# 384 columns of the down weights as a transfer with eight source stretches, and TensorE's loop waits held by its matmuls

## The chip, the cores and the metric

The kernel runs on one core of a Trainium2 chip. The core has a matrix engine (TensorE, PE in the profile, with its weight loads listed apart as PEld), a vector engine (VectorE, DVE), a scalar engine (ScalarE, ACT), GpSimd (POOL) and a sequencer that issues transfers (SyncE, SP). Sixteen DMA engines move data from the chip's main memory (HBM) into the on-chip buffer (SBUF); TensorE writes its results to PSUM. The engines run at once and order their work by counting semaphores. The metric is the device time of one execution in microseconds (us), less is better.

## The reference

One token is decoded through a layer: attention over a long cache, then a gated feed-forward block, each behind a layer norm and with a residual sum. Everything is float32.

```python
# D = 640, H = 32 heads, Sk = 8192 cached positions, Dh = 192, F = 1536
def _A_ref(x, k_cache, v_cache, wq, wo):
    q = (x @ wq) per head
    scores = einsum("bhqd,bhkd->bhqk", q, k_cache) * Dh ** -0.5
    p = softmax(scores)
    o = einsum("bhqk,bhkd->bhqd", p, v_cache)
    return o @ wo

def _B_ref(x, W_gate, W_up, W_down):
    gate = x @ W_gate
    h = gate * (gate > 0) * (x @ W_up)
    return h @ W_down

h  = x + _A_ref(layernorm(x), k_cache, v_cache, wq, wo)
h2 = h + _B_ref(layernorm(h), W_gate, W_up, W_down)
```

The caches of keys and values alone are 32 x 8192 x 192 x 4 bytes each, 403 MB together, and each byte is used once.

## The kernel before

The host packs every input into rows of 128 partitions (`pack`), in the order in which they are used, so that one transfer brings several things at once: a head's keys, values, columns of the query weights and rows of the output weights. Three large SBUF slots, X, Y and Z, take them.

**The loop.** After a first head's keys (`row_p`), ten turns of three heads each run. A turn uses five transfers, `row_1` to `row_5`, of 7.6 to 8.2 MB, which SP issues in `sync_program` (line 581): into X, Z, Y, X and Y. Before it issues one, it waits until the slot's old contents are used; TensorE, DVE and ACT report this on the semaphores `free`. `free[3]` lets the turn's last load into Y go (line 590). It takes two increments: one from the matmul of value block 23 of the turn's second head, and one that TensorE's sequencer sends after it has seen that DVE is done with Y (lines 250 to 252). A landed transfer adds 16 to its semaphore `land`.

**One head.** TensorE's part is `pe_unit` (line 226). It multiplies the head's keys by the query in two halves (`pe_k`, line 190), corrects the head before by its softmax sum (`pe_o`, `pe_l`), multiplies the values by the probabilities in 32 blocks (`pe_v`, line 197), makes the query of the next head (`pe_q`, line 206) and transposes a maximum (`pe_t`). ACT copies results out of PSUM and takes the exponential, and counts up `a2p` three times a head; DVE makes the softmax's maxima and the products with weights, and counts up `d2p` twice. `pe_unit` waits for these with `wait` (line 136): an instruction of its own on TensorE's sequencer, which takes what it waited for off the semaphore again. `op` (line 142) can hang a wait or an increment on a matmul instead. The waits for transfers (`landed`) are instructions of their own too.

**The tail.** After the last turn come the last head, the output product, the second layer norm, and the feed-forward block. Its weights arrive as `row_up`, `row_gate` and, by line 609, `row_down` in four pieces d0 to d3. The down weights are 12 rows of D = 640 columns on each partition, and the pieces are cut by `DOWN` (line 35):

```python
DOWN = ((0, 6 * D), (6 * D, 10 * D), (10 * D, 11 * D + D // 2), (11 * D + D // 2, 12 * D))
```

TensorE's last loop (line 326) goes over these rows j: it waits for d0 ahead of row 0, d1 ahead of row 6, d2 ahead of row 10, and d3 ahead of the second half of row 11. Rows 0 to 5 also need the first half of the transposed activations `guT`, which DVE makes (lines 503 and 505). `pe_fill` (line 258) is a matmul into an unused place, which keeps TensorE going ahead of a wait; one stands ahead of row 6. After the last row, ACT and DVE copy the result out of PSUM and SP stores it, as two rows of 320.

Of the kernel before, what the change touches and what calls it, by code (L numbers as in the profile page):

```python
# [11 lines left out]
DJ, FJ = D // P, F // P  # L12
# [19 lines left out]
W_T2B = 16 * PW  # L32
W_T3 = 16 * PW + OW
W_UP = DJ * F
DOWN = ((0, 6 * D), (6 * D, 10 * D), (10 * D, 11 * D + D // 2), (11 * D + D // 2, 12 * D))


def pack(inputs):
    import numpy as np
    order = np.arange(D).reshape(2, 2, DG).transpose(1, 0, 2).reshape(D)  # L40
    x = np.ascontiguousarray(inputs["A_x"]).reshape(D)[order].reshape(P, DJ)
    kc = np.ascontiguousarray(inputs["A_k_cache"])[0]
    vc = np.ascontiguousarray(inputs["A_v_cache"])[0].reshape(H, P, KW)
    wq = np.ascontiguousarray(inputs["A_wq"])[order].reshape(P, DJ, H, DH)
    wo = np.ascontiguousarray(inputs["A_wo"])[:, order].reshape(H, DH, D)

    def kt(h):
        k = kc[h].reshape(4, 32, 32, 2, DH).transpose(4, 3, 0, 2, 1).reshape(DH, 2, 4, 2, 512)
        a = k[:P]
        b = k[P:].transpose(1, 0, 2, 3, 4).reshape(P, 4, 2, 512)  # L50
        r = np.stack([a[:, 0], a[:, 1], b], 1)
        return r.transpose(0, 3, 1, 2, 4).reshape(P, KW)

    def qw(h):
        return wq[:, :, h].reshape(P, QW)

    def ow(h):
        w = wo[h]
        mid = w[DH - P:P]
        full = np.concatenate([w[:DH - P], w[P:]], 0)  # L60
        return np.concatenate([full, np.concatenate([mid[:, 0:D // 2], mid[:, D // 2:]], 0)], 1)

    cat = lambda *a: np.concatenate(a, 1)
    kw = [kt(h) for h in range(H)]
    out = {"row_p": cat(qw(0), kw[0], qw(1), x, np.zeros((P, W_P - 2 * QW - KW - DJ), np.float32))}
    rows = [np.empty((NTURN, P, w), np.float32) for w in (W_1, W_2, W_3, W_4, W_5)]
    for i in range(NTURN):
        a, b, c = 3 * i + 1, 3 * i + 2, 3 * i + 3
        va, vb, vv = vc[a - 1], vc[b - 1], vc[c - 1]
        rows[0][i] = cat(kw[a], va[:, :8 * PW], qw(b))  # L70
        rows[1][i] = cat(va[:, 8 * PW:], ow(a - 1), kw[b][:, :12 * 512])
        rows[2][i] = cat(kw[b][:, 12 * 512:], qw(c), vb[:, :24 * PW])
        rows[3][i] = cat(vb[:, 24 * PW:], kw[c])
        rows[4][i] = cat(ow(b - 1), ow(c - 1), qw(c + 1), vv)
    for n, r in enumerate(rows):
        out[f"row_{n + 1}"] = r
    h = H - 1
    out["row_t1"] = cat(kw[h], vc[h - 1][:, :8 * PW])
    out["row_t2a"] = cat(vc[h - 1][:, 8 * PW:], ow(h - 1))
    out["row_t2b"] = np.ascontiguousarray(vc[h][:, :16 * PW])  # L80
    out["row_t3"] = cat(vc[h][:, 16 * PW:], ow(h))
    out["row_up"] = np.ascontiguousarray(inputs["B_W_up"])[order].reshape(P, DJ * F)
    out["row_gate"] = np.ascontiguousarray(inputs["B_W_gate"])[order].reshape(P, DJ * F)
    down = np.ascontiguousarray(inputs["B_W_down"])[:, order].reshape(4, FJ, 32, D).transpose(0, 2, 1, 3).reshape(P, FJ, D)
    last = down[:, FJ - 1].reshape(P, 4, 2, DG // 2).transpose(0, 2, 1, 3).reshape(P, D)
    out["row_down"] = cat(down[:, :FJ - 1].reshape(P, (FJ - 1) * D), last)
    return {k: np.ascontiguousarray(v) for k, v in out.items()}


def build(nc, arrays):  # L90
# [51 lines left out]
    def op(ins, w=None, inc=None):  # L142
        if w is not None:
            ins._wait_ge(*w)
        if inc is not None:
            ins.then_inc(inc, 1)
        return ins
# [39 lines left out]

    te = nc.tensor

    def pe_k(blk, half):  # L190
        for part in range(3):
            for g in range(4):
                m = te.matmul(sc[Q(g), half * 512:half * 512 + 512], qs[:, 32 * part:32 * part + 32],  # L193
                              blk(half, part * 4 + g), start=(part == 0), stop=(part == 2))
        op(m, inc=p2d)

    def pe_v(blk, i0, i1, last=None, inc_at=None):
# [5 lines left out]
            if i == 31 and last is not None:  # L203
                op(m, inc=last)

    def pe_q():
        te.matmul(q_ps[:, 0:96], prod[:, 0:P], pat[:, 0, :], start=True, stop=False)  # L207
        te.matmul(q_ps[0:64, 0:96], prod[:, P:DH], pat[:, 1, :], start=False, stop=True)
        op(te.matmul(q_ps[64:P, 0:96], prod[:, P:DH], pat[:, 2, :], start=False, stop=True), inc=p2a)  # L209

# [12 lines left out]
    def pe_l(w=None):  # L223
        op(te.matmul(pl[:, 0:1], ones, vec["rs"], start=True, stop=True), w, inc=p2d)  # L224

    def pe_unit(kblk, vblk, rows, freed=None, freed_at=None, o_first=False):
        def landed(n):
            if n in rows:
                s, sub = rows[n]
                wait(te, s, 16, sub)  # L230

        wait(te, a2p, 1, 1)
        if o_first:
            wait(te, a2p, 1, 1)
            pe_o()
        landed("k0")
        pe_k(kblk, 0)
        if not o_first:
            wait(te, a2p, 1, 1)
            pe_o()  # L240
        wait(te, a2p, 1, 1)
        pe_l()
        landed("k1")
        pe_k(kblk, 1)
        landed("v0")
        at = None if freed is None else (freed_at, freed)
        pe_v(vblk, 0, 8, inc_at=at)
        landed("v8")
        pe_v(vblk, 8, 24, inc_at=at)
        wait(te, d2p, 2, 2)  # L250
        if freed is free[3]:
            te.sem_inc(freed, 1)
        pe_q()
        pe_t()
        landed("v24")
        pe_v(vblk, 24, 32, last=p2a)
# [4 lines left out]
    def tensor_program():  # L261
# [11 lines left out]
        wait(te, d2p, 2, 2)  # L273
        pe_q()
        pe_t()
        def first():
            pe_unit(ka, va, {"k0": (land[1], 16), "v8": (land[2], 16)}, free[1], 7, o_first=True)

        def rest():
            pe_unit(kb, vb, {"k1": (land[3], 16), "v24": (land[4], 16)}, free[3], 23)  # L280
            pe_unit(kc, vcc, {"v0": (land[5], 0)})

        turns(ET.PE, first, rest)
        pe_o((a2p, 2))
        pe_l((a2p, 3))
        wait(te, tl["t2b"], 16, 16)
        pe_v(vz, 0, 16)
        for g in range(4):
            op(te.matmul(acc[Q(g), 0:DG], ones[:, 0:32], accs[:, g * DG:(g + 1) * DG], start=True, stop=False),
               None if g else (d2p, 3))  # L290
        for g in range(4):
            r = slice(0, 64) if g < 2 else slice(64, P)
            te.matmul(acc[Q(g), 0:DG], ones[r, 0:32], accs[r, D + (g % 2) * DG:D + (g % 2 + 1) * DG],
                      start=False, stop=False)
        wait(te, tl["t3"], 16, 16)
        pe_v(vz, 16, 32, last=p2a)
        pe_o((a2p, 4))
        for g in range(4):
            op(te.matmul(acc[Q(g), 0:DG], oc[:, 0:1].to_broadcast([P, 32]), woz[:, g * DG:(g + 1) * DG],
                         start=False, stop=False), None if g else (d2p, 5))  # L300
        for g in range(4):
            r = slice(0, 64) if g < 2 else slice(64, P)
            m = te.matmul(acc[Q(g), 0:DG], oc[r, 1:2].to_broadcast([64, 32]),
                          woz[r, D + (g % 2) * DG:D + (g % 2 + 1) * DG], start=False, stop=True)
        m.then_inc(p2a, 1)
        op(te.matmul(pt[:, 0:1], ones, vec["hs1"], start=True, stop=True), (a2p, 5), inc=p2d)
        op(te.matmul(od[:, 0:1], ones, vec["hs2"], start=True, stop=True), (d2p, 6), inc=p2d)
        wait(te, tl["up"], 16, 16)
        for j in range(DJ):
            for g in range(4):  # L310
# [9 lines left out]
        op(m, inc=p2d)  # L320
        te.matmul(q_ps[:, 0:DG], ident, h4, start=True, stop=False)
        pe_fill(128)
        wait(te, a2p, 5, 5)
        wait(te, tl["d0"], 16, 16)
        wait(te, d2p, 7)
        for j in range(FJ):
            if j == 6:
                pe_fill(512)
                wait(te, d2p, 8, 8)
                wait(te, tl["d1"], 16, 16)  # L330
            if j == 10:
                wait(te, tl["d2"], 16, 16)
            if j < FJ - 1:
                for g in range(4):
                    te.matmul(q_ps[Q(g), 0:DG], guT[:, j, :], down[:, j * D + g * DG:j * D + (g + 1) * DG],  # L335
                              start=False, stop=False)
            else:
                for half in range(2):
                    if half:
                        wait(te, tl["d3"], 16, 16)  # L340
                    for g in (2, 3, 0, 1):
                        at = j * D + half * (D // 2) + g * (DG // 2)
                        m = te.matmul(q_ps[Q(g), half * (DG // 2):(half + 1) * (DG // 2)], guT[:, j, :],  # L343
                                      down[:, at:at + DG // 2], start=False, stop=bool(half))
                        if half and g == 3:
                            op(m, inc=p2a)
# [231 lines left out]
    def load(t, src, s):  # L578
        sp.dma_start(t, src).then_inc(s, 16)

    def sync_program():
# [24 lines left out]
        load(Y[:, W_T3:W_T3 + W_UP], dram["row_up"], tl["up"])  # L606
        wait(sp, free[1], 1, 1)
        load(X[:, 0:W_UP], dram["row_gate"], tl["gate"])
        for n, (a, b) in enumerate(DOWN):
            load(X[:, W_UP + a:W_UP + b], dram["row_down"][:, a:b], tl[f"d{n}"])  # L610
        wait(sp, fout, 2)
        load(out[0, 0].rearrange("(g n) -> g n", g=2), o2[31:33, :], out_s)
        wait(sp, fout, 2, 2)
# [22 lines left out]
```

## Time and profile before

| | |
|---|---|
| median of 3 runs | 1037.62 us (1037.56 to 1037.63) |
| the profiled execution | 1037.69 us |
| its span, first to last instruction | 1036.4 us |
| mean clock granted to TensorE | 0.76 of full |
| bytes moved by DMA in the span | 446.05 MB, 430 GB/s |

The profile is of one execution, 0.07 us above the median. Its busy times are those of work proper; waits, branches and the issuing of transfers count as idle. A letter q behind an engine (PEq) means its sequencer. L137 is line 137 of the kernel, the wait instruction inside `wait`; a row that names it as what ended an idle time means that the engine stood at such a wait, and the cause lies behind it. TensorE's float32 matmul is listed as two passes, so that the numbers of matmuls in the rows are twice those in the code.

### The profile page before, as it was taken

What the parts mean: (1) busy time and instruction counts of PE and PEld (TensorE: products, weight loads), DVE (VectorE), ACT (ScalarE), POOL (GpSimd) and SP (SyncE); (2) the same over time, 40 slices, a digit from 0 to 9 for tenths busy, and PEclk for the clock granted to TensorE, in tenths of its full rate; (3) what the DMA queues carried; (4) which work ended last, traced back from release to release, by engine and by line L of the source; (5) the groups of instructions that cost most, each with busy time, mean ns of one, the idle gap of its engine ahead of it and who ended that gap; (6) DMA issues with size and microseconds to landing.
All of it is one profiled execution on the core that took longest, in us unless ns stands there. A gap on an engine that the chain in (4) does not pass through costs nothing. (4 is left out here: it accounts for less than half of the span.)

```text
span 1036.4 us, 10124 instructions
## 1 busy us (share of the span) xinstructions
PE 549.5 (53%) x4374; PEld 185.5 (18%) x4374; DVE 196.0 (19%) x517; ACT 41.7 (4%) x139; POOL 1.5 (0%) x13
## 2 busy tenths in 40 slices
PE   0745546446364463564654636546455455464577
PEld 0211212111121121121211202111111111121123
DVE  1311211121222022121211210221222012111221
ACT  1000000000000000000000000000000000000000
POOL 0000000000000000000000000000000000000000
PEclk9877867768777677687676877867778778677788
DMA  9999999999999999999999999999999999999998
GB/s 403 442 435 421 434 438 432 441 421 438 427 451 416 436 445 437 416 441 437 438 421 442 431 438 435 421 438 441 427 425 438 439 423 434 438 432 444 420 425 352
DMA packets 8796, 446.05 MB, mean 430 GB/s; under 512 B 979, under 2 KB 1109, under 8 KB 1237
## 3 DMA queue, kind: packets, MB, share of 16 engines
q1 hardware_dynamic: 8788, 445.95, 99.6%
q8 instruction: 6, 0.10, 0.0%
q14 instruction: 2, 0.01, 0.0%
HBM read 445.94 MB, written 0.00 MB: 430 GB/s over the span
## 5 line engine op out<-in xcount | busy, mean ns | idle before, releaser
L193 PE MATMUL sc<-slot_x,qs 128*32 128x512 f32 x1008 | 150.7, 742 | 93.2 <-PEq L137 93.2
L200 PE MATMUL po<-slot_y,p 128*2 128x384 f32 x1152 | 118.2, 562 | 80.6 <-DMA slot_y<-row 76.8
L200 PE MATMUL po<-slot_z,p 128*2 128x384 f32 x560 | 72.0, 667 | 100.2 <-PEq L137 100.2
L193 PE MATMUL sc<-slot_y,qs 128*32 128x512 f32 x288 | 53.5, 905 | 83.0 <-PEq L137 83.0
L200 PE MATMUL po<-slot_x,p 128*2 128x384 f32 x336 | 43.6, 652 | 86.6 <-PEq L137 86.6
L406 DVE STREAM_TRANSPOSE st<-sc 128x512 f32<-128x512 f32 x64 | 45.6, 713 | 160.7 <-PE sc L193 160.7
L193 PEld LDWEIGHTS sc<-slot_x,qs 128*32 128x32 f32 x1008 | 36.7, 134 | 175.8 <-issue 175.5
L200 PEld LDWEIGHTS po<-slot_y,p 128*2 128x2 f32 x1152 | 31.0, 94 | 165.4 <-DMA slot_y<-row 85.9
L393 DVE COPY oc<-od 64x2 f32<-64x2 f32 x33 | 5.0, 151 | 246.6 <-PE od L218 246.6
L412 DVE TENSOR_REDUCE m<-pt 128x1 f32<-128x128 f32 x32 | 9.3, 292 | 185.6 <-PE pt L212 185.6
L200 PEld LDWEIGHTS po<-slot_z,p 128*2 128x2 f32 x560 | 15.2, 102 | 146.5 <-issue 145.2
L524 ACT COPY qs<-q_ps 128x96 f32<-128x96 f32 x33 | 7.9, 239 | 793.8 <-PE q_ps L209 793.8
L218 PE MATMUL od<-mrl,ob 128*128 128x1 f32 x264 | 35.2, 254 | 8.5 <-PEq L137 7.3
L218 PEld LDWEIGHTS od<-mrl,ob 128*128 128x128 f32 x264 | 32.8, 195 | 34.5 <-issue 31.2
L387 DVE SCALAR_TENSOR_TENSOR prod<-slot_y,xn,prod 128x192 f32<-128x192 f32 x88 | 36.9, 419 | 3.1
L193 PEld LDWEIGHTS sc<-slot_y,qs 128*32 128x32 f32 x288 | 12.7, 154 | 112.2 <-issue 112.2
L401 DVE RECIPROCAL rl<-pl 128x1 f32<-128x1 f32 x32 | 5.4, 168 | 134.1 <-PE pl L224 133.5
L200 PEld LDWEIGHTS po<-slot_x,p 128*2 128x2 f32 x336 | 9.0, 94 | 109.6 <-issue 109.6
L193 PE MATMUL sc<-slot_z,qs 128*32 128x512 f32 x240 | 27.6, 592 | 0.0
L527 ACT COPY ob<-po 128x384 f32<-128x384 f32 x32 | 15.3, 479 | 155.6 <-PE po L200 155.6
L207 PE MATMUL q_ps<-pat,prod 128*128 128x96 f32 x66 | 15.8, 322 | 7.1 <-PEq L137 7.1
L385 DVE TENSOR_SCALAR prod<-slot_y,xn 128x192 f32<-128x192 f32 x22 | 6.9, 315 | 64.7 <-DMA slot_y<-row 64.7
(97 smaller groups left out, 248.7 us busy)
## 6 DMA issues: line engine op xcount, KB each, us to landing
slot_x<-row SPq DMA_DIRECT2D x10, 8160.0 KB, 26.6
slot_z<-row SPq DMA_DIRECT2D x10, 8160.0 KB, 45.4
slot_y<-row SPq DMA_DIRECT2D x10, 8160.0 KB, 45.4
slot_x<-row SPq DMA_DIRECT2D x10, 7680.0 KB, 46.6
slot_y<-row SPq DMA_DIRECT2D x10, 7584.0 KB, 27.2
slot_x<-row_t SPq DMA_DIRECT2D x1, 7680.0 KB, 26.1
slot_y<-row_p SPq DMA_DIRECT2D x1, 7136.0 KB, 19.7
slot_z<-row_t2a SPq DMA_DIRECT2D x1, 5088.0 KB, 37.7
```

Of the source, the lines that this page charges most:

```text
L193: m = te.matmul(sc[Q(g), half * 512:half * 512 + 512], qs[:, 32 * part:32 * part + 32], blk(half, part * 4 + g), start=(part == 0), stop=( ...
L200: m = te.matmul(po[32 * g:32 * g + 2, 0:PW], p[:, 2 * i:2 * i + 2], blk(i), start=(i < 4), stop=(i >= 28))
L207: te.matmul(q_ps[:, 0:96], prod[:, 0:P], pat[:, 0, :], start=True, stop=False)
L218: m = te.matmul(od[:, part:part + 1], ob[:, at:at + P], mrl[:, k:k + 1], start=(k == 0), stop=(k == 1))
L385: dv(ve.tensor_scalar(prod, w3[:, 0, :], xn[:, 0:1], None, op0=ALU.mult), w=first)
L387: dv(STT(prod, w3[:, j, :], xn[:, j:j + 1], prod, op0=ALU.mult, op1=ALU.add), w="self", inc=d2p if j == DJ - 1 else None)
L393: dv(ve.tensor_copy(oc[0:64], od[0:64, 0:2]), w=pd(), inc=inc)
L401: dv(ve.reciprocal(vec["rl"], pl[:, 0:1]), w=pd())
L406: return dv(ve.transpose(st[:, s], sc[:, s]), w=w)
L412: dv(ve.reduce_max(vec["m1"], pt[:, 0:P], axis=AX.X, negate=True), w=pd(), inc=d2a)
L524: op(ac.copy(qs, q_ps[:, 0:96]), w=ap("p2a"), inc=a2p)
L527: op(ac.copy(ob, po[:, 0:PW]), w=ap("p2a"), inc=a2p)
```

## The change

The edit has two parts.

**The down weights.** The first 384 of the columns that d1 brought (row 6 of the down weights, columns 0 to 383) leave `row_down`. They are packed as an array `row_u` of its own, with eight rows: each holds the 384 columns of 16 partitions, one after the other, and 16 floats of filling, so that the eight rows are separate stretches of memory. One new transfer reads them as 8 x 16 x 384 and writes them to the same place in X, [128, 384], as before. It is issued between `row_gate` and d0. It counts on d1's semaphore, so TensorE waits for 32 there in place of 16. d1 is shorter by the same columns; d2 and d3 keep their size, and only their place in `row_down` moves.

**TensorE's waits in the loop.** The waits for `a2p` and `d2p` in `pe_unit` become waits held by the matmul that needs them. They no longer take off what they waited for; the counts go up through a turn (`seen`), and at the end of a turn two waits take the nine and the six off. The increment of `free[3]` moves from the sequencer to the first matmul of `pe_q`. The numbers in the tail's waits follow from the counts of the last head. No matmul is added, taken away or reordered.

```diff
-DOWN = ((0, 6 * D), (6 * D, 10 * D), (10 * D, 11 * D + D // 2), (11 * D + D // 2, 12 * D))
+W_U = 384
+DOWN = ((0, 6 * D), (6 * D + W_U, 10 * D), (10 * D, 11 * D + D // 2), (11 * D + D // 2, 12 * D))
...
-    out["row_down"] = cat(down[:, :FJ - 1].reshape(P, (FJ - 1) * D), last)
+    down = cat(down[:, :FJ - 1].reshape(P, (FJ - 1) * D), last)
+    out["row_down"] = cat(down[:, :6 * D], down[:, 6 * D + W_U:])
+    eight = np.zeros((8, 16 * W_U + 16), np.float32)
+    eight[:, :16 * W_U] = down[:, 6 * D:6 * D + W_U].reshape(8, 16 * W_U)
+    out["row_u"] = eight
...
-        wait(te, a2p, 1, 1)
+        n = seen["a2p"]
         if o_first:
-            wait(te, a2p, 1, 1)
-            pe_o()
-        landed("k0")
-        pe_k(kblk, 0)
-        if not o_first:
-            wait(te, a2p, 1, 1)
-            pe_o()
-        wait(te, a2p, 1, 1)
-        pe_l()
+            pe_o((a2p, n + 2))
+            landed("k0")
+            pe_k(kblk, 0)
+        else:
+            pe_k(kblk, 0, (a2p, n + 1))
+            pe_o((a2p, n + 2))
+        pe_l((a2p, n + 3))
+        seen["a2p"] += 3
+        seen["d2p"] += 2
...
-        wait(te, d2p, 2, 2)
-        if freed is free[3]:
-            te.sem_inc(freed, 1)
-        pe_q()
+        pe_q((d2p, seen["d2p"]), freed if freed is free[3] else None)
...
             pe_unit(kc, vcc, {"v0": (land[5], 0)})
+            for n, s in (("a2p", a2p), ("d2p", d2p)):
+                wait(te, s, seen[n], seen[n])
+                seen[n] //= 3
...
-                wait(te, tl["d1"], 16, 16)
+                wait(te, tl["d1"], 32, 32)
...
         load(X[:, 0:W_UP], dram["row_gate"], tl["gate"])
+        load(X[:, W_UP + 6 * D:W_UP + 6 * D + W_U], dram["row_u"][:, 0:16 * W_U].rearrange("a (b n) -> a b n", b=16),
+             tl["d1"])
         for n, (a, b) in enumerate(DOWN):
-            load(X[:, W_UP + a:W_UP + b], dram["row_down"][:, a:b], tl[f"d{n}"])
+            at = a - W_U if n else a
+            load(X[:, W_UP + a:W_UP + b], dram["row_down"][:, at:at + b - a], tl[f"d{n}"])
```

More of the change, by code (lines that the diff above doesn't have):

```diff
@@ L188, in build, with pe_k @@
     te = nc.tensor
-    def pe_k(blk, half):
+    def pe_k(blk, half, w=None):
         for part in range(3):
@@ L194, in pe_k @@
                               blk(half, part * 4 + g), start=(part == 0), stop=(part == 2))
+                if part == 0 and g == 0:
+                    op(m, w)
         op(m, inc=p2d)
@@ L204, in pe_v, with pe_q @@
                 op(m, inc=last)
-    def pe_q():
-        te.matmul(q_ps[:, 0:96], prod[:, 0:P], pat[:, 0, :], start=True, stop=False)
+    def pe_q(w=None, inc=None):
+        op(te.matmul(q_ps[:, 0:96], prod[:, 0:P], pat[:, 0, :], start=True, stop=False), w, inc)
         te.matmul(q_ps[0:64, 0:96], prod[:, P:DH], pat[:, 1, :], start=False, stop=True)
@@ L224, in pe_l @@
         op(te.matmul(pl[:, 0:1], ones, vec["rs"], start=True, stop=True), w, inc=p2d)
+    seen = {"a2p": 0, "d2p": 0}
     def pe_unit(kblk, vblk, rows, freed=None, freed_at=None, o_first=False):
@@ L281, in rest @@
             pe_unit(kc, vcc, {"v0": (land[5], 0)})
+            for n, s in (("a2p", a2p), ("d2p", d2p)):
+                wait(te, s, seen[n], seen[n])
+                seen[n] //= 3
         turns(ET.PE, first, rest)
-        pe_o((a2p, 2))
-        pe_l((a2p, 3))
+        pe_o((a2p, 5))
+        pe_l((a2p, 6))
         wait(te, tl["t2b"], 16, 16)
@@ L289, in tensor_program @@
             op(te.matmul(acc[Q(g), 0:DG], ones[:, 0:32], accs[:, g * DG:(g + 1) * DG], start=True, stop=False),
-               None if g else (d2p, 3))
+               None if g else (d2p, 5))
         for g in range(4):
@@ L296, in tensor_program @@
         pe_v(vz, 16, 32, last=p2a)
-        pe_o((a2p, 4))
+        pe_o((a2p, 7))
         for g in range(4):
             op(te.matmul(acc[Q(g), 0:DG], oc[:, 0:1].to_broadcast([P, 32]), woz[:, g * DG:(g + 1) * DG],
-                         start=False, stop=False), None if g else (d2p, 5))
+                         start=False, stop=False), None if g else (d2p, 7))
         for g in range(4):
@@ L305, in tensor_program @@
         m.then_inc(p2a, 1)
-        op(te.matmul(pt[:, 0:1], ones, vec["hs1"], start=True, stop=True), (a2p, 5), inc=p2d)
-        op(te.matmul(od[:, 0:1], ones, vec["hs2"], start=True, stop=True), (d2p, 6), inc=p2d)
+        op(te.matmul(pt[:, 0:1], ones, vec["hs1"], start=True, stop=True), (a2p, 8), inc=p2d)
+        op(te.matmul(od[:, 0:1], ones, vec["hs2"], start=True, stop=True), (d2p, 8), inc=p2d)
         wait(te, tl["up"], 16, 16)
@@ L322, in tensor_program @@
         pe_fill(128)
-        wait(te, a2p, 5, 5)
+        wait(te, a2p, 8, 8)
         wait(te, tl["d0"], 16, 16)
-        wait(te, d2p, 7)
+        wait(te, d2p, 9)
         for j in range(FJ):
@@ L328, in tensor_program @@
                 pe_fill(512)
-                wait(te, d2p, 8, 8)
-                wait(te, tl["d1"], 16, 16)
+                wait(te, d2p, 10, 10)
+                wait(te, tl["d1"], 32, 32)
             if j == 10:
```

## The prediction

> **What bounds the kernel now.** I read the page's busy shares first, then its queue shares, then who waited for whom, and last the ending in order of time.
>
> ```profile
> PE 549.5 (53%) x4374; PEld 185.5 (18%) x4374; DVE 196.0 (19%) x517; ACT 41.7 (4%) x139; POOL 1.5 (0%) x13
> ...
> q1 hardware_dynamic: 8788, 445.95, 99.6%
> q8 instruction: 6, 0.10, 0.0%
> ```
>
> No compute engine is busy for much more than half of the span, while the one data queue fills 99.6% of what 16 DMA engines have in 1036.4 us. The kernel streams 446 MB and the rest hides behind it. The rate of one engine follows: 445.95 MB over (16 x 0.996 x 1036.4 us) is 27.0 KB per us. TensorE's waits confirm it:
>
> ```profile
> PE po L200 <- PEq L137: 190.6, 22, 10.3
> PE sc L193 <- PEq L137: 176.2, 21, 9.9
> PE po L200 <- DMA slot_y<-row: 76.8, 10, 8.2
> ```
>
> Columns are us in total, times, longest. Line 137 is the helper that writes a wait as an instruction of its own; the 43 long ones, up to 10 us, stand ahead of scores (line 193) and value products (line 200) whose block has not landed. TensorE idles for over 440 us, so what it saves in a turn only lengthens the next wait.
>
> Only the two ends of the stream can then move the time. The end, in order of time (start, duration):
>
> ```profile
> 1029.75 0.38 DVE L505 STREAM_TRANSPOSE guT<-gu 128x192 f32<-128x192 f32 x1
> 1029.78 1.54 PEld L335 LDWEIGHTS q_ps<-slot_x,guT 128*32 128x32 f32 x48 [0.64 <-DVE guT L505]
> 1029.81 1.84 PE L335 MATMUL q_ps<-slot_x,guT 128*32 128x160 f32 x48 [0.47 <-PEq L137]
> 1031.57 0.30 PEld L259 LDWEIGHTS po<-accs,ones 128*128 128x128 f32 x2 [0.25 <-issue]
> 1031.57 1.13 PE L259 MATMUL po<-accs,ones 128*128 128x512 f32 x2
> 1032.86 1.00 PEld L335 LDWEIGHTS q_ps<-slot_x,guT 128*32 128x32 f32 x32 [0.99 <-issue]
> 1032.89 1.63 PE L335 MATMUL q_ps<-slot_x,guT 128*32 128x160 f32 x40 [0.19 <-PEq L137]
> 1034.02 0.19 PEld L335 LDWEIGHTS q_ps<-slot_x,guT 128*32 128x32 f32 x8 [0.15 <-issue]
> 1034.18 0.43 PEld L343 LDWEIGHTS q_ps<-slot_x,guT 128*32 128x32 f32 x16
> 1034.32 0.48 PE L343 MATMUL q_ps<-slot_x,guT 128*32 128x80 f32 x16
> ```
>
> And the landings of the pieces of the down weights, from their issues (KB, us from issue to landing; the four were issued one after the other from 989.2):
>
> ```profile
> 989.22 1.86 SPq L579 DMA_DIRECT2D slot_x<-row_down  x4
> ```
>
> ```profile
> slot_x<-row_down SPq DMA_DIRECT2D x1, 1920.0 KB, 40.5
> slot_x<-row_down SPq DMA_DIRECT2D x1, 1280.0 KB, 43.1
> slot_x<-row_down SPq DMA_DIRECT2D x1, 480.0 KB, 43.7
> slot_x<-row_down SPq DMA_DIRECT2D x1, 160.0 KB, 43.7
> ```
>
> With issues about 0.47 us apart (1.86 over four), the pieces land at 1029.7 (d0), 1032.8 (d1), 1033.9 (d2) and 1034.3 (d3). The products of rows 0 to 5 start at 1029.78, when DVE hands over guT; rows 6 to 9 start at 1032.86, on d1; row 10 at 1034.02, on d2, after a gap of 0.15. So three landings pace the last 2 us. What makes them late is seen in the share of the DMA engines at work near the end (us, busy time and count by engine, clock, DMA share, GB/s):
>
> ```profile
> 1030.00:1031.00 1.00, 1.00 (x36) 1.00 (x32) 0.12 (x1) 0.00 (x0) 0.00 (x0) 1.00 0.93 381
> 1031.00:1032.00 1.00, 1.00 (x21) 0.62 (x14) 0.00 (x0) 0.00 (x0) 0.00 (x0) 1.00 0.86 337
> 1032.00:1032.50 0.50, 0.50 (x2) 0.00 (x0) 0.00 (x0) 0.00 (x0) 0.00 (x0) 1.00 0.39 154
> 1032.50:1033.00 0.50, 0.31 (x5) 0.14 (x8) 0.00 (x0) 0.00 (x0) 0.00 (x0) 1.00 0.34 136
> 1033.00:1033.50 0.50, 0.50 (x20) 0.50 (x23) 0.00 (x0) 0.00 (x0) 0.00 (x0) 1.00 0.20 74
> 1033.50:1034.00 0.50, 0.50 (x22) 0.36 (x12) 0.00 (x0) 0.00 (x0) 0.00 (x0) 1.00 0.04 15
> ```
>
> The share falls from 0.86 to 0.39 at 1032 and then trickles: some 6 of the 16 engines are still at work at 1032.2, three at 1033.2, one at 1033.7. Each engine has the same bytes; a few are up to 2 us behind, and a transfer has landed when its last engine has.
>
> **The change, part by part.**
>
> *The transfer of 384 columns.* It takes 128 x 384 x 4 = 196,608 bytes out of d1 (1280 KB becomes 1088) and brings them between gate and d0, so the bytes stay. What matters is which engines carry them. Two views bear on that, the window of the output's store and the window in which d1, d2 and d3 land:
>
> ```profile
> DMA packets 5, 0.02 MB, mean 9 GB/s; under 512 B 2, under 2 KB 4, under 8 KB 4
> ```
>
> ```profile
> DMA packets 327, 0.91 MB, mean 206 GB/s; under 512 B 47, under 2 KB 175, under 8 KB 302
> ...
> q1 hardware_dynamic: 327, 0.91, 51.7%
> ```
>
> The store has two rows, and two packets under 512 B, the semaphore writes; three loads of 128 rows have 47, near 16 each. So the number of engines seems to follow the outermost count, and I take eight engines for a source of eight stretches (an estimate; the bounds are two and 16). On them the 196,608 bytes are 24.6 KB or 0.91 us each, where every engine carried 12.3 KB or 0.455 us. Small packets cost extra: the window is 4.4 us long, 51.7% of 16 engines are 36.4 us, and 0.91 MB at 27.0 KB per us are 33.7, so some 280 packets of data pay about 10 ns each; 16 pieces of 1536 bytes add 0.16. The eight end 0.455 + 0.16 = **0.61 us later**, the other eight **0.455 us sooner**. At two engines, each carries 98 KB (3.64 us) in 64 pieces (0.64) and ends 3.8 us later; at 16, everything ends 0.08 us later.
>
> [...]
>
> Which half are the laggards in? If the last engine does not carry the piece, d1, d2 and d3 land 0.455 sooner: 1032.3, 1033.45, 1033.85. Then TensorE is late next: the filler of line 259 ends at 1032.70, so rows 6 to 9 begin 0.16 sooner, the 0.15 ahead of row 10 goes, and d3 is there in time. That is **-0.3 us**, up to -0.455 if the filler gives way sooner. If the last engines do carry it, d0 lands 0.91 + 0.16 later, at 1030.8 for 1029.7; rows 0 to 5 start 1.0 late, the filler ends at 1033.7, rows 6 to 9 begin 0.85 later and the 0.15 is saved: **+0.7 us**. No row numbers the engines, so the choice between these ends is nearly open. I take -0.3, with less than half of the chance: the one engine still at work after 1033.5 decides, and if it doesn't carry the piece, up to 0.455 comes free before another can take its place; the other end needs that engine among the carriers.
>
> SP issues one more transfer ahead of the down weights; such an issue took 0.43 us. They land 40 us after issue, behind a full queue: nothing. Should the queue stand empty, it is 0.43.
>
> *TensorE's waits.* A turn has 17 waits and one increment as instructions of their own. Twelve of the waits (three of a2p and one of d2p in each of three units) and the increment go into matmuls, and two settling waits are added: 11 sequencer instructions fewer. From the waits' own row:
>
> ```profile
> L137 PEldq EVENT_SEMAPHORE  x182: 51/51/51, 2.4 to 1034.3; - x182
> ```
>
> At 51 ns that is 0.56 us a turn, all in stretches that end in a wait for a block. I cost it at nothing; uncovered it would be 5.6 us over ten turns, either gained or, if a held wait stalled the weight loads behind it as long, lost. Behind a held wait stand the same matmuls, in the same order, that stood behind the separate one; DVE and ACT wait for those.
>
> The moved increment frees slot Y for the turn's last load: now it fires when the first matmul of line 207 ends, not before it starts.
>
> ```profile
> 839.06 0.46 PE L207 MATMUL q_ps<-pat,prod 128*128 128x96 f32 x2
> 839.39 0.33 SPq L579 DMA_DIRECT2D slot_y<-row  x1
> 849.19 0.14 PEld L200 LDWEIGHTS po<-slot_x,p 128*2 128x2 f32 x8 [9.29 <-issue]
> 860.09 0.33 SPq L579 DMA_DIRECT2D slot_x<-row  x1
> 867.05 0.11 PEld L200 LDWEIGHTS po<-slot_y,p 128*2 128x2 f32 x8 [8.21 <-DMA slot_y<-row]
> ```
>
> At most 0.46 us later, against 849.19 - 839.39 = 9.8 us in which the queue still carries the load before. The shortest cover in the turn is that of slot X, issued 7.0 us ahead of the landing at 867.05. Nothing, therefore.
>
> The shorter program can shift the instruction fetches. The store's window shows one:
>
> ```profile
> q8 instruction: 1, 0.02, 3.0%
> ```
>
> 3.0% of 16 engines over 2 us is 0.96 us of one engine; the span has six, which can be part of why engines lag. One fewer or more on the last engine is up to -1 or +1 us; with eleven instructions gone of a loop that has hundreds I take it at nothing.
>
> The sum against the profiled execution, 1037.69 us (span 1036.4 and 1.3 around it): -0.3 gives 1037.4; the median, 1037.62, is 0.07 lower, so **1037.3 us**.
>
> **The rivals.**
>
> 1. *The last engines carry the piece.* Slower, by 0.7: 1038.3. For it: nothing excludes it, and d0 has no spare time (1029.7 against 1029.78).
> 2. *Laggards in both halves.* The last one gains, and another, some 0.3 to 0.6 us ahead of it, is pushed past: -0.1 to +0.3, about 1037.8. For it: three engines still work at 1033.2. [...]
> 3. *The piece is spread over all 16 engines* after all, its target having 128 rows: +0.08, 1037.7; the change does not do what it says.
> 4. *Slower: the stream runs dry at slot X or Y*, because a held wait delays TensorE's part of the release. It decides from 7.0 us of delay on; each 0.2 us a turn past that is 2 us in ten turns, 1039.7. Against it: the order of the work is unchanged, and the one known delay is 0.46.
> 5. *Faster by 11 waits a turn*: 5.6 us less, 1032.0. Against it: 99.6% on the queue, which no wait of TensorE fills further.
>
> **How the numbers follow.** No change within 0.2% (2.1 us, about what a measurement of this kernel can tell) holds my forecast, 0.45, and rivals 1, 2 and 3 with 0.22, 0.18 and 0.08: 0.93. Slower: rival 4 and a piece on two engines (+3.8), 0.04. Faster: rival 5, 0.03. The range takes in -0.455 with 0.07 of scatter, and rival 1 with as much: 1037.1 to 1038.4. Forecast and rivals 1 to 3 lie in it.
>
> **What would show it.** Right: the queue's share stays near 99.6%; TensorE's long waits for blocks stay as they are, and only the short ones ahead of lines 207 and 218 change their releaser from line 137 to ACT or DVE; the DMA share from 1032 to 1034 falls to nothing sooner, and the gap before row 10 is gone. A window around the new piece's landing has eight packets under 512 B more if eight engines carry it, 16 if rival 3 holds. Rows 0 to 5 that wait for d0 until 1030.5 or later mean rival 1; a stretch of the queue below 0.9 in mid-span means rival 4; a span under 1034 means rival 5. I am wrong if a fetch of instructions moves onto another engine, or if eight stretches don't mean eight engines.

## The result, and the profile after

| | before | after |
|---|---|---|
| median of 22 runs each | 1037.62 us | 1039.32 us |
| range | 1037.12 to 1039.23 | 1038.15 to 1040.77 |
| profiled execution | 1037.69 us | 1038.92 us |
| span | 1036.4 us | 1037.7 us |

The changed kernel is slower, by 1.7 us in the medians; the ratio over all runs is 1.0013, with a 95% interval of 1.0007 to 1.0019. In size this is inside the 0.2% that the prediction called no change, but the median lies 0.9 us above the top of the forecast range, and the move is up, where 0.3 us down was forecast. Six of the 22 runs lie at 1038.15 to 1038.35 and the others at 1038.92 or more; the one trace kept is of the upper group, so what sets the six apart stays open. The profiled execution is 0.4 us quicker than the median, so the trace shows 1.23 of the 1.7 us.

The page of the changed kernel first, the lines that answer to those quoted of before:

```profile
PE 551.7 (53%) x4374; PEld 185.0 (18%) x4374; DVE 196.0 (19%) x517; ACT 41.7 (4%) x139; POOL 1.5 (0%) x13
...
q1 hardware_dynamic: 8924, 445.95, 99.6%
q8 instruction: 6, 0.10, 0.0%
```

Nothing has moved in the large: the same work, the same bytes, the same number of instruction fetches, and a queue that is busy for 99.6% of the span. The waits of TensorE for blocks are as they were too (line 142 is now the wait instruction):

```profile
PE po L207 <- PEq L142: 188.0, 23, 10.6
PE sc L198 <- PEq L142: 174.1, 21, 9.4
PE po L207 <- DMA slot_y<-row: 79.7, 10, 8.5
```

The end in order of time shows the difference:

```profile
1029.99 0.38 DVE L515 STREAM_TRANSPOSE guT<-gu 128x192 f32<-128x192 f32 x1
1031.32 1.54 PEld L345 LDWEIGHTS q_ps<-slot_x,guT 128*32 128x32 f32 x48 [1.93 <-DVE guT L515]
1031.35 1.84 PE L345 MATMUL q_ps<-slot_x,guT 128*32 128x160 f32 x48 [1.77 <-PEq L142]
1033.11 0.30 PEld L265 LDWEIGHTS po<-accs,ones 128*128 128x128 f32 x2 [0.25 <-issue]
1033.12 1.12 PE L265 MATMUL po<-accs,ones 128*128 128x512 f32 x2
1034.17 1.24 PEld L345 LDWEIGHTS q_ps<-slot_x,guT 128*32 128x32 f32 x40 [0.76 <-issue]
```

```profile
slot_x<-row_down SPq DMA_DIRECT2D x1, 1920.0 KB, 41.9
```

The second fence is d0 in the view of the issues: issued at 989.3, it lands at 1031.2, where it landed at 1029.7 before. The weight loads of rows 0 to 5 are put down to DVE, but they need only the first half of guT, and even the second was begun at 1029.99 and took 0.38; they start at 1031.32, 0.1 us behind d0. The kernel before shows the same order, though the prediction read its start at 1029.78 as DVE's:

```profile
1029.09 0.38 DVE L505 STREAM_TRANSPOSE guT<-gu 128x192 f32<-128x192 f32 x1
```

The first half of guT was done at 1029.47, d0 landed at 1029.7, and the rows began 0.1 us behind it. So they waited for d0 before as well, and d0's delay now starts them 1.54 us later. From there TensorE runs without a pause: the filler ends and rows 6 to 10 follow at once (x40 in one piece, at 1034.17), with none of the gap ahead of row 10. The 1.54 us shrink by the idle pieces of before (0.19 and 0.15) to about 1.2 at the end.

Why is d0 late? The view of stretches, with the same columns as in the prediction, before (first fence) and after (second):

```profile
1018.00:1022.00 4.00, 4.00 (x32) 1.30 (x28) 0.39 (x3) 0.00 (x0) 0.00 (x0) 0.54 1.00 426
1022.00:1026.00 4.00, 2.54 (x26) 0.79 (x18) 0.00 (x0) 0.58 (x1) 0.00 (x0) 1.00 0.94 396
1026.00:1030.00 4.00, 3.52 (x48) 1.75 (x42) 1.23 (x4) 0.00 (x0) 0.00 (x0) 1.00 0.98 414
1030.00:1034.00 4.00, 3.81 (x82) 2.62 (x74) 0.12 (x1) 0.00 (x0) 0.00 (x0) 1.00 0.57 227
```

```profile
1018.00:1022.00 4.00, 4.00 (x36) 1.15 (x28) 0.51 (x4) 0.00 (x0) 0.00 (x0) 0.67 1.02 434
1022.00:1026.00 4.00, 1.86 (x14) 0.64 (x14) 0.00 (x0) 0.58 (x1) 0.00 (x0) 1.00 0.99 306
1026.00:1030.00 4.00, 3.58 (x40) 1.67 (x32) 0.98 (x4) 0.00 (x0) 0.00 (x0) 1.00 0.95 397
1030.00:1034.00 4.00, 2.65 (x50) 1.84 (x50) 0.37 (x1) 0.00 (x0) 0.00 (x0) 1.00 0.80 323
```

Look at the last two columns, the share of the DMA engines' time and the rate. From 1022 to 1026, when the new piece is under way, the engines are as busy as ever (0.99), but move 306 GB/s in place of 396. Busy engines at three quarters of the rate: packets take longer, those of d0 664 ns in the mean for 577 before. The missing 90 GB/s over 4 us are 0.36 MB, or 0.84 us at 430 GB/s. The packet records of the two traces, summed for the time after 1018 us, say which packets:

```
piece                 bytes  packets  alone     before   after    lost after
end of up and gate    30720   63      1142 ns   1 slow    6 slow    2.7 us
the new piece          1536  128        65 ns    -       84 slow    2.8 us
d0                    15360  128       577 ns   0 slow   56 slow   11.1 us
d1, d2, d3              all  128 each     -       0 slow    0 slow    -
```

(Packets are counted in the changed kernel. "Alone" is the usual time of a packet that nothing slows, 577 ns being d0's mean before and 65 ns the shortest of the new piece; "slow" is over 1.1 times that; "lost" is the sum over the packets.) In both traces one slow packet of up and gate begins as a fetch of instructions ends. The slow packets of d0 begin between 1022.6 and 1026.4. In all 16.6 us of engine time are lost, about 1.0 us for each of 16 engines, and most of it by packets of d0 while the new piece is under way.

### The profile page after: what moved, and what is told of

The parts are those of the page before. It is cut to its first block, busy times and chain, and to the rows that moved or that the text cites. A ratio compares the mean times of both kernels' runs of the same rounds, so it can differ in the third digit from the quotient of the medians.

```text
span 1037.7 us, 10011 instructions
## 1 busy us (share of the span) xinstructions
PE 551.7 (53%) x4374; PEld 185.0 (18%) x4374; DVE 196.0 (19%) x517; ACT 41.7 (4%) x139; POOL 1.5 (0%) x13
## 3 DMA queue, kind: packets, MB, share of 16 engines
q1 hardware_dynamic: 8924, 445.95, 99.6%
## 5 line engine op out<-in xcount | busy, mean ns | idle before, releaser
L198 PE MATMUL sc<-slot_x,qs 128*32 128x512 f32 x1008 | 147.1, 726 | 88.3 <-PEq L142 88.3
L207 PE MATMUL po<-slot_y,p 128*2 128x384 f32 x1152 | 125.9, 592 | 84.7 <-DMA slot_y<-row 79.7
L207 PE MATMUL po<-slot_z,p 128*2 128x384 f32 x560 | 67.6, 633 | 102.0 <-PEq L142 102.0
L198 PE MATMUL sc<-slot_y,qs 128*32 128x512 f32 x288 | 57.1, 956 | 85.8 <-PEq L142 85.8
```

Source lines behind the costliest of these rows:

```text
L207: m = te.matmul(po[32 * g:32 * g + 2, 0:PW], p[:, 2 * i:2 * i + 2], blk(i), start=(i < 4), stop=(i >= 28))
```

## The experiments

Two theories: **collision**, the eight engines write where other engines write, and both are slowed; and **lag**, the eight include the engines that are last anyway, and nobody is slowed. Rivals outside of these are TensorE's held waits, small pieces as such, and reads at odd addresses. Each time stands beside the kernel before on the same chip; ratios have 95% intervals.

**TensorE's part alone.** The diff is that of the change without the hunks that name `W_U` or `row_u`.

> TensorE's held waits as in the change, the down weights as before. If the time comes from the transfer (theories 'collision' and 'lag'), this is the time of before, 1037.6 us within 0.3. If the held waits cost something, about 1039.3.

1037.48 us against 1037.65, ratio 0.9999 (0.9990 to 1.0008). The held waits cost nothing that shows. The wait instructions on TensorE's sequencer fall from 182 to 78, in this run (first line) as in the changed kernel (second):

```profile
L137 PEldq EVENT_SEMAPHORE  x78: 51/51/51, 2.4 to 1034.2; - x78
L142 PEldq EVENT_SEMAPHORE  x78: 51/51/51, 2.4 to 1035.4; - x78
```

**The transfer alone.** The hunks with `W_U` and `row_u`, on the kernel before.

> The transfer of eight stretches as in the change, TensorE's waits as before. Both theories of the transfer give the whole change, 1038.2 to 1039.7; if the waits are the cause, 1037.6.

1039.24 us against 1037.65, ratio 1.0016 (1.0007 to 1.0025). These 1.6 us are the whole loss, as far as the intervals can tell.

**The same piece on 16 engines.**

```diff
-    eight = np.zeros((8, 16 * W_U + 16), np.float32)
-    eight[:, :16 * W_U] = down[:, 6 * D:6 * D + W_U].reshape(8, 16 * W_U)
+    eight = np.zeros((P, W_U + 16), np.float32)
+    eight[:, :W_U] = down[:, 6 * D:6 * D + W_U]
...
-dram["row_u"][:, 0:16 * W_U].rearrange("a (b n) -> a b n", b=16)
+dram["row_u"][:, 0:W_U]
```

> The change with a source of 128 rows for the same 384 columns: same bytes, same pieces of 1536 bytes, same place in the queue, but on 16 engines. 'Collision' (the eight engines write where other engines write and slow them) and 'lag' (the eight include the last engines) both give the time of before, 1037.6 to 1037.8. If the small pieces or the further transfer cost the time, it stays at 1038.5 to 1039.5, and pieces of 1536 bytes then take near 87 ns here too.

1037.66 us against 1037.65, ratio 0.9999 (0.9990 to 1.0008). Small pieces and one more transfer cost nothing that shows; all 128 packets of 1536 bytes take 65 to 67 ns. The two windows from 1022 to 1026, changed kernel first, this one second:

```profile
DMA packets 212, 1.23 MB, mean 306 GB/s; under 512 B 24, under 2 KB 152, under 8 KB 152
```

```profile
DMA packets 241, 1.55 MB, mean 387 GB/s; under 512 B 32, under 2 KB 160, under 8 KB 160
```

Both hold the 128 small data packets (152 less 24, 160 less 32). The packets under 512 bytes are the semaphore writes: 16 for gate and 8 for the new piece with eight stretches, 16 and 16 with 128 rows. By this count eight engines carry the piece from eight stretches and 16 that from 128 rows, as the prediction estimated.

**Stretches at multiples of 256 bytes.**

```diff
-    eight = np.zeros((8, 16 * W_U + 16), np.float32)
+    eight = np.zeros((8, 16 * W_U + 64), np.float32)
```

> The change with 64 floats of filling behind each stretch in place of 16, so that every stretch starts at a multiple of 256 bytes. If reading from odd addresses is what slows the packets, 1037.3 to 1038.3; under 'collision' and 'lag' as the change, 1039.3.

1039.04 us against 1037.65, ratio 1.0012 (1.0002 to 1.0021), 298 GB/s from 1022 to 1026. So stretches that start off a multiple of 256 bytes are not the cause.

That leaves collision and lag. To part them, the kernel before gets one further load of 196,608 bytes of zeros into a spare buffer that nothing reads, in four forms with the same bytes and place in the queue:

```diff
         load(X[:, 0:W_UP], dram["row_gate"], tl["gate"])
+        load(spare, dram["row_x"][:, 0:6144].rearrange("a (b n) -> a b n", b=16), sp_s)
         for n, (a, b) in enumerate(DOWN):
```

Sixteen engines, `row_x` of 128 rows:

> The kernel before with one further load of 196,608 bytes of zeros between gate and d0, into a spare buffer that nothing reads: 128 rows, 16 engines. A measure for the next three. Bytes alone are 0.455 us an engine and eight pieces more are 0.08: 1038.2 us under every theory, and about 395 GB/s from 1022 to 1026.

1038.23 us against 1037.65, ratio 1.0005 (0.9995 to 1.0014), 391 GB/s: the price of the bytes, as worked out.

Eight stretches into all 128 partitions, as in the diff above:

> The kernel before with the same further load, but from eight stretches into all 128 partitions. 'Lag' alone: 0.91 us of bytes and 0.16 of pieces on eight engines, 1038.0 to 1038.7. 'Collision': the 1.6 us of the change and the 0.455 that it did not take elsewhere, 1039.3 to 1039.9, with near 295 GB/s from 1022 to 1026.

1039.50 us, ratio 1.0018 (1.0008 to 1.0027), 293 GB/s.

Eight stretches into half of the partitions (`spare[0:64]` or `spare[64:128]`, 768 columns, `b=8`):

> The same further load, eight stretches, same bytes, but into partitions 0 to 63 only, 768 columns wide. If the collision is with whatever serves a partition and the eight engines are those that serve partitions 0 to 63 anyway, they only get in each other's way and the other eight run on: 1038.0 to 1039.0. If it doesn't matter where they write, as the load into all 128 partitions.

> As the load into partitions 0 to 63, but into 64 to 127. Under 'collision' by target the eight engines all write where the other eight do, which is the worst case: 1039.8 to 1041, the other eight slowed most. If it doesn't matter where they write, the same time as into partitions 0 to 63.

1040.14 us, ratio 1.0023 (1.0014 to 1.0033), 279 GB/s for the lower half; 1040.54 us, ratio 1.0026 (1.0016 to 1.0036), 248 GB/s for the upper. The expectation for the lower half was missed by over 1 us: the load into partitions 0 to 63 is as bad as into all. The intervals of the two halves overlap, so they don't tell the theories apart by time. A half may be too coarse: with 64 partitions each stretch goes to eight neighbours, and if other loads have some of these written by another engine, the engines collide inside the half as well. That is a guess, as no trace gives the partitions of an engine. The next pair therefore gives each stretch four partitions, and takes one engine to a stretch.

Four partitions to a stretch (`spare[0:32]` and `spare[64:96]`, 1536 columns, `b=4`):

> The kernel before with a further load of 196,608 bytes of zeros from eight stretches into partitions 0 to 31 alone, 1536 columns wide, four partitions to an engine. Theory 'collision by target': if engine e serves partitions 4e to 4e+3 in every load, each of the eight writes only where it writes anyway, and no packet is slowed: rate from 1022 to 1026 near 390 GB/s, time 1037.7 to 1038.6 (0.95 us more on eight engines, as far as those are the last ones). Rival 'the eight stretches themselves' (source, or few engines): 1039.3 to 1040.2 and under 320 GB/s, as in the other loads on eight engines.

> As the load into partitions 0 to 31, but into 64 to 95. 'Collision by target': each of the eight writes where one engine of the other half writes: 1039.5 to 1041 and under 300 GB/s. Rival 'the eight stretches themselves': the same time as into 0 to 31.

1038.59 us against 1037.70, ratio 1.0009 (1.0000 to 1.0018), for partitions 0 to 31; 1040.64 us, ratio 1.0028 (1.0018 to 1.0039), for 64 to 95. The source, the number of engines, the size of the packets and the place in the queue are the same; only the target differs, by 64 partitions. The stretches of 1022 to 1026 and 1026 to 1030, 0 to 31 first:

```profile
1022.00:1026.00 4.00, 2.29 (x18) 0.80 (x18) 0.00 (x0) 0.58 (x1) 0.00 (x0) 1.00 0.94 395
1026.00:1030.00 4.00, 3.16 (x36) 1.51 (x28) 1.36 (x4) 0.00 (x0) 0.00 (x0) 1.00 0.98 415
```

```profile
1022.00:1026.00 4.00, 1.95 (x14) 0.42 (x6) 0.00 (x0) 0.58 (x1) 0.00 (x0) 1.00 0.94 252
1026.00:1030.00 4.00, 3.26 (x40) 1.44 (x40) 0.00 (x0) 0.00 (x0) 0.00 (x0) 1.00 0.96 366
```

395 GB/s, the rate of before, against 252 at the same share of busy time. In the packet records, none of d0's 128 packets is slow for 0 to 31; for 64 to 95, 68 are, at 850 ns in the mean. The load's own packets, of 6144 bytes, take 235 ns in the mean for 0 to 31 and 377 ns for 64 to 95. Eight stretches and eight engines as such slow nothing, at 395 GB/s; where the eight write does, at 252. Partitions 64 to 95 are not slow in themselves: the piece on 16 engines writes them too, at 65 to 67 ns a packet.

The reading that fits is that the eight engines write partitions 0 to 31 in other loads too, and that 64 to 95 are other engines'. The two runs agree with it, at 395 and 252 GB/s and with none and 68 of d0's packets slowed, but it is the author's reading and not shown: no trace here gives an engine's number.

**Twice the columns.** `W_U = 768`.

> The change with 768 columns in place of 384. If the loss goes by the bytes that collide, twice the 1.65 us of the change: 1040.5 to 1041.5. If it is a fixed price for such a transfer, 1039.0 to 1039.6.

1041.57 us against 1037.70, ratio 1.0042 (1.0029 to 1.0055): 3.9 us, where twice the loss of the change (1.7 us, or 1.6 for the transfer alone; 1.65 is taken) is 3.3. So the loss grows with the bytes; the interval, 3.0 to 5.7 us, takes in exact proportion. The time falls just above the range that was expected. The rate is low for longer:

```profile
1022.00:1026.00 4.00, 1.22 (x6) 0.30 (x2) 0.00 (x0) 0.58 (x1) 0.00 (x0) 1.00 0.96 254
1026.00:1030.00 4.00, 3.71 (x32) 1.73 (x36) 0.00 (x0) 0.00 (x0) 0.00 (x0) 0.65 0.98 325
```

**The further load 35 us earlier.** The line of the diff above stands behind the load of `row_t2b`.

> The kernel before with the further load of eight stretches into all 128 partitions, issued 35 us earlier, between the loads of rows t2b and t3. If the DMA engines' time that is lost cannot be had back on a full queue, as at the end: 1039.2 to 1039.9. If the loss counts only because the end of the stream is near, 1038.2.

1039.56 us, ratio 1.0017 (1.0007 to 1.0026), as at the end (1039.50). The dip is now at 996 to 1000:

```profile
996.00:1000.00 4.00, 3.40 (x35) 1.78 (x37) 0.66 (x4) 2.27 (x5) 0.00 (x0) 1.00 0.95 292
```

So the engine time that was lost here was not had back in the 35 us that followed on a full queue.

## Why the prediction was wrong

*What bounds the kernel* holds. The queue binds at 99.6%, TensorE has time to spare in the loop, and only engine time and the end of the stream move the total.

*TensorE's waits at nothing*: right, by the run with that part alone. The moved increment and the further issue show nothing either: that run, and the piece on 16 engines, which has both, are at the time of before. The fetches of instructions are six, as before, and the piece on 16 engines, whose program differs in that transfer alone, loses nothing.

*Eight engines for eight stretches*: right, by the count of semaphore writes (8 for eight stretches, 16 for 128 rows).

*The eight engines 0.61 us later, the other eight 0.455 us sooner*: this is the step that failed. It gave every packet its time alone, and so took for granted that it harms no one where an engine writes. In place of 8 x 577 ns, an engine's share of d0 took 8 x 664 ns in the mean, and the new piece's packets 87 ns where 16 pieces in 1.07 us make 67. Over all 16 engines 1.0 us each is lost, where eight were to gain 0.455. That packets could be slowed by it was in none of the rivals. The 27.0 KB per us and engine came from loads of 128 rows into 128 partitions; no row showed eight engines writing all 128, and the cost of that should have stood open on the upper side. The forecast's own sign came out the other way: the share of the DMA engines' time from 1030 to 1034 rose from 0.57 to 0.80, where its end was to fall to nothing sooner.

*Rows 0 to 5 start "when DVE hands over guT"*: misread, since they waited for d0. The sum hardly changes by it: in rival 1 the rows would start 1.07 us late in place of 1.0.

*Which half are the laggards in*: the side taken was wrong too. The load into partitions 0 to 31 slows none of d0's packets, and gives the eight 0.95 us more; the median rises by 0.89 us (0 to 1.9 by the interval). In its trace the rows wait for d0 too, the first half of guT being done at 1029.30:

```profile
1030.58 1.84 PE L338 MATMUL q_ps<-slot_x,guT 128*32 128x160 f32 x48 [1.41 <-PEq L140]
```

They start 0.8 us later than before (1029.81), with none of d0's packets slowed. So the engines that end last are among the eight, or near enough to be pushed past: rival 1. Its sign, rows 0 to 5 waiting for d0 beyond 1030.5, is in the trace of the change too (1031.32), but there it proves nothing, since the slowed packets delay d0 as well.

*The sum*: the further load into all partitions, 1.85 us above before, less that into 0 to 31, 0.89 above, puts the collision at 0.96 us. The remaining 0.7 of the change's 1.65 is what rival 1 was priced at, 0.7. These two differences are of runs in two groups, each against its kernel before, and each is uncertain by about a microsecond; the split is a consistent reading, not a measurement to a tenth.

*The range* reached to rival 1 at 1038.4 and so was short by about the collision alone.

A version that beats the kernel before is not in sight from this: as far as the run with 0 to 31 goes, the eight engines that a source of eight stretches selects include those that end last, or come close to them, and none of the runs gave the other eight more to do.

## What to carry to other kernels

On a full DMA queue, a transfer's count of bytes need not be its price: look at the rate beside the busy share, and where the share stays and the rate falls (0.99 of the time at 306 GB/s here, for 0.94 at 396), packets take longer, and their records say which. Before load is shifted between engines, try where the transfer writes: here eight engines on partitions 0 to 31 slowed nothing (395 GB/s from 1022 to 1026, where the kernel before has 396), and on 64 to 95, 0 to 63, 64 to 127 or all 128 they did (252, 279, 248 and 293). And engine time lost 35 us ahead of the end was paid as fully as at the end (1039.56 us for 1039.50), so on such a queue a small experiment need not stand at the very end to be read.

## What the runs showed of the hardware that was not expected

Where a load of eight stretches writes decides whether it and the loads beside it are slowed. With four partitions to an engine, into 64 to 95, packets of d0 (15,360 bytes) took 850 ns in the mean where they were slowed (68 of 128), for 577 before, and the load's own took 377 ns; into 0 to 31 none was slowed, and the load's own took 235 ns. That the first are other engines' partitions is a reading that no trace confirms by an engine's number.

SP's issue of the changed kernel's last piece took long:

```profile
L589 SPq DMA_DIRECT2D slot_x<-row_down x4: 411/432/5202, 989.3 to 990.7; - x4
```

The other three took 0.41 to 0.43 us, the last 5.2 us (columns: shortest, median, longest in ns). The traces of all six kernels in which eight stretches go into all 128 partitions have it, 5.2 to 5.9 us, also the one with the load 35 us earlier; in the other eight, with 16 engines or with fewer pieces to a stretch, the same issue took 0.43 us. It is not what costs the time: the piece landed 44 us after its issue, and the loads into 64 to 95 and into either half lose 2.5 to 2.9 us without it. Why it takes so long is not shown.
